# A gated mix of a long convolution and dilated window attention on one core: 64-key by 57-query attention blocks, k and v loaded once, gate in result order, q scaled on VectorE, two-pass last stage

## The chip, the cores and the metric

One core of a Trainium2 chip runs the kernel. The metric is device microseconds of one execution; the kernel before has a median of 310.66 us over three runs (309.36 to 315.1). Its engines are named as in the profile: PE (TensorE matmul) and PEld (TensorE weight load), DVE (VectorE), ACT (ScalarE), POOL (GpSimd), SP (the queue that issues most DMAs).

## What is computed

Everything is bf16, S = 2048 rows, D = 640 columns, 32 heads of 20.

```python
g = sigmoid((x * gate_w).sum(-1, keepdims=True))        # x = A_q
k_shift = sum over lag j = 0..3 of k[n - j] * shift_k[:, j]
kv = k_shift * v
y  = irfft(rfft(pad(kv)) * rfft(pad(ssm_k)))[:S] + kv * ssm_D
a  = x * y
q, k, v = split_heads(x @ wqkv)                         # 32 heads of 20
# row s attends to rows s, s-2, ..., s-14 (W = 8, dilation 2); rows below 0 are masked
o  = softmax(q . k * 20**-0.5) . v
b  = o @ wo
out = g * a + (1 - g) * b
```

## The kernel before: tiling, staging and order

**Attention.** Dilation 2 splits the rows into even and odd ones; each half becomes a window of 8 neighbours. `transposes` writes x transposed into `xT`, the even half and then the odd half, each with 7 rows of zeros ahead. The 2062 columns are cut into 17 blocks of 128 keys and 121 queries (`NB`, `BP`). `vproj` projects v per block (L428) into `VW` with a column of ones (or zeros, `valid`) per head, which gives the softmax sum. `qkproj` projects q and k for 128 features at a time (`ft` 0 to 4, `w` 0 for q and 1 for k; L479), copies them to a staging tile `stg` (two of them, one for q and one for k), and `fragger` copies each head's 20 rows from there by DMA (L513) into `kb` and `qb`, four heads to a tile, where 11 more rows hold a mask in factored form; there are three such pairs of tiles, so the pair of head group t waits until group t-3 has been scored. `score_gen` (L537) multiplies `kb` and `qb` block by block into PSUM, one head's scores on 128 partitions; ACT takes the exponential into `ET` (L544); `pv_gen` (L569) multiplies by `VW`, and DVE divides by the sums (L581, L583) into `oS`.

**Convolution.** `conv` on DVE (L389 to L399) makes kv from k and v, which `loads` brings in four pieces of 16 rows by 160 columns (runs of 320 bytes), reusing two k buffers and one v buffer. The FFT is matrix products: stage 1 (`s1_unit`, L600) and stage 2 (`s2_unit`, L618), first of the filter `h_lin` (`h_stream`) and then of kv (`u_stream`), in five column groups of 16 (`NG`, `IL`); `swaps` and `mults` form the complex product on DVE (L711, L714), `inverse1` is the first inverse stage (L728) into `Cm`, and `final` the last (L811), three time slots of 16 at once. `final` then multiplies by `qg` (L819), which is x times g, adds `bl`, which is (1-g)b from `outproj` (L751, L767, L772), with L822, and writes out (L824).

**Gate.** 80 matmuls (L441) give the gate with rows in `xT`'s order; it goes through a DRAM scratch (L450 to L454) to come back in the result's row order as `g_nat`, and `omg` is 1-g.

**Buffers that tie stages.** `oS` takes the place of `xS`; `wo` that of `Wv`; `h_lin` that of `kvin` (the raw k and v), and later `oT`; `qg` that of `kv`, so `qg` loads only when the last stage-1 product of kv has been issued (event `us1`). `h_stream` starts after the `h_lin` loads, the last q/k projection, the last `conv` piece and the gate matmuls, since its tiles lie where `xT`, `Wqk` and `stg` were.

**Order.** A planner (`Plan`) simulates all the streams with assumed costs while the program is built and so fixes the order on each engine: it picks the request that can start first, plus 120 ns per priority step. PE is shared by all stages; PSUM has four slots; DMAs of `loads` and `fragger` stand in one order on SP. POOL's own start-up work (`pool_head`) is in program order: memsets, DMAs of small constants, 24 DMAs of mask rows into `kb` and `qb` (L373, L374).

Of the kernel before, what the change touches and what calls it, by code (L numbers as in the profile page):

```python
# [17 lines left out]
S = 2048  # L18
D = 640
L = 4096  # L20
H = 32
# [4 lines left out]
BP = 121  # L26
NB = 17
# [5 lines left out]
OW = 2062  # L33
KW = 128 * NB
QW = BP * NB
GROUPS = [[0, 1, 2, 3], [4, 5, 6, 7], [8, 9, 10], [11, 12, 13], [14, 15, 16]]
PARTS = [((0, 1), [(0, 8)]), ((2, 3, 4), [(8, 5), (13, 4)])]

NG = 5
IL = 16  # L40

# [5 lines left out]
def fft_consts():  # L47
# [20 lines left out]
    for b in range(64):  # L68
# [4 lines left out]
    return dict(F1b=_np_bf16(F1b.reshape(128, 128)), G=_np_bf16(G), M=_np_bf16(M.reshape(128, 256)),  # L73
                T=_np_bf16(T))


def attn_consts():
    B, C = 256.0, 512.0
    kk = np.arange(128); qq = np.arange(BP)
    kc = kk // 8 - 8; ko = kk % 8; qc = qq // 8 - 8; qo = qq % 8  # L80
    sk = np.where(kc % 2 == 0, 1.0, -1.0); sq = np.where(qc % 2 == 0, 1.0, -1.0)
    mk = np.zeros((NF, 128)); mq = np.zeros((NF, BP))
    mk[0] = kc * kc; mk[1] = kc; mk[2] = 1.0
    mq[0] = -B; mq[1] = B * (2 * qc + 1); mq[2] = -B * (qc * qc + qc) - C / 2
    for v in range(8):
        mk[3 + v] = sk * (ko == v)
        mq[3 + v] = (C / 2) * sq * np.where(v < qo, -1.0, 1.0)
    tot = np.einsum("fk,fq->kq", mk, mq)
    dlt = kk[:, None] - qq[None, :]
    inb = (dlt >= 0) & (dlt <= 7)  # L90
    assert (tot[inb] == 0).all() and (tot[~inb] <= -C / 2).all()
    for m in (mk, mq):
        assert (_np_bf16(m).astype(np.float64) == m).all()
    pos = BP * np.arange(NB)[None, :] - PRE + kk[:, None]
    valid = (((pos >= 0) & (pos < 1024)) | ((pos >= HS) & (pos < HS + 1024))).astype(np.float32)
    return dict(mk=_np_bf16(np.tile(mk, (1, NB))), mq=_np_bf16(np.tile(mq, (1, NB))),
                valid=_np_bf16(valid), ident=_np_bf16(np.eye(128)))
# [28 lines left out]
class Req:  # L126


    def __init__(self, engs, cost=0.0, deps=(), take=0, give=(), n=0, move=0.0, pri=None):
        self.engs, self.cost, self.deps, self.take, self.give, self.n, self.move = engs, cost, deps, take, give, n, move  # L130
        self.pri = pri


LAT = {("P", "A"): 230.0, ("P", "D"): 230.0, ("A", "P"): 120.0, ("D", "P"): 120.0, ("A", "D"): 100.0, ("D", "A"): 100.0}


class Plan:


    def __init__(self, nslots):  # L140
        self.at = dict(P=0.0, A=0.0, D=0.0, G=0.0, S=0.0)
        self.pipe = 0.0
        self.lane = {"S": [], "G": []}
        self.slots = [Bank() for _ in range(nslots)]
        self.streams = []

# [3 lines left out]
    def cost(self, r, e):  # L150
        if r.n:
            return 190.0 + 0.834 * r.n if e == "A" else 150.0 + 1.05 * r.n
        return r.cost[e] if isinstance(r.cost, dict) else r.cost

    def start(self, r, e):
        t = self.at[e]
        for d in r.deps:
# [6 lines left out]
        if r.move and len(self.lane[e]) >= 8:  # L164
            t = max(t, self.lane[e][-8])
        return t
# [4 lines left out]
    def run(self):  # L171
        while self.streams:
# [9 lines left out]
            assert pick is not None, [s[2].engs for s in self.streams]  # L182
# [5 lines left out]
            self.at[e] = end  # L188
            if r.move:
# [8 lines left out]
            for s in r.give:  # L198
                self.slots[s].free = Ev(end, e)
            try:  # L200
# [6 lines left out]
def kernel(  # L207
# [41 lines left out]
    kvin = p0.tile([128, 2 * 19 * 160 + 16 * 160], BF, name="kvin", tag="H")  # L249
    kv = p0.tile([128, 2, 64, 80], BF, name="kv", tag="kv")  # L250
    G = p0.tile([128, 32, 2, 128], BF, name="G")
    Dz = p0.tile([128, 160], BF, name="Dz")
    F1b = p0.tile([128, 128], BF, name="F1b")
    M = p0.tile([128, 2, 128], BF, name="M")
    g_nat = p0.tile([128, 16], F32, name="g_nat")
    omg = p0.tile([128, 16], F32, name="omg")
    g_chk = p0.tile([128, 16], F32, name="g_chk")
    dpool = ctx.enter_context(tc.tile_pool(name="scratch_dram", bufs=1, space=DRAM))
    g_scr = dpool.tile([S], F32, name="g_scr")
    valid = p0.tile([128, NB], BF, name="valid")  # L260
    wg = p0.tile([128, NDT], BF, name="wg")
    rds = []
    for e in range(2):
        rdb = p0.tile([128, 3, 32], F32, name=f"rd{e}")
        rds.append(rdb)
# [3 lines left out]
    VW = pR.tile([128, NB, H, 21], BF, name="VW")  # L269
# [5 lines left out]
    NET = 8  # L275
    for e in range(NET):
        ETb = pR.tile([128, 2, 512], BF, name=f"ET{e}")
        ETs.append(ETb)
    Lx = ExitStack()
# [3 lines left out]
    pa = pL.tile([128, 16, 160], BF, name="pa")  # L283
    pb = pL.tile([128, 16, 160], BF, name="pb")
    wraw = pL.tile([128, 160, 4], BF, name="wraw")
    wl = pL.tile([128, 4, 160], BF, name="wl")
# [3 lines left out]
    kin = [kvin[:, 3040 * e:3040 * e + 3040].rearrange("p (n c) -> p n c", n=19) for e in range(2)]  # L290
    vin = kvin[:, 6080:8640].rearrange("p (n c) -> p n c", n=16)
# [12 lines left out]
    def us(nbytes, run):  # L304
        return nbytes / 16.0 / run * (10.0 + run / 24.0)
# [3 lines left out]
    def loads():  # L309
        def load(name, dst, src, nb, run, deps=()):  # L310
            g = yield Req("S", 60.0, deps, move=us(nb, run))
# [3 lines left out]
        def load_x(c):  # L315
            yield from load(f"x{c}", xS[:, 4 * c:4 * c + 4, :], xq4[:, c // 2, 4 * (c % 2):4 * (c % 2) + 4, :], 655360, 1280)

        def load_kv(a):
            dk = [ev(f"conv{a - 2}")] if a >= 2 else []
            dv = [ev(f"conv{a - 1}")] if a >= 1 else []  # L320
            for q in range(4):
                lo = 3 if a == 0 else 0
                n0 = 16 * a - 3 + lo
                yield from load(f"k{a}{q}", kin[a % 2][32 * q:32 * q + 32, lo:19, :],
                                raw(k2, n0 * D + 160 * q, [[64 * D, 32], [D, 19 - lo], [1, 160]]), 32 * 19 * 320, 320, dk)
            for q in range(4):
                yield from load(f"v{a}{q}", vin[32 * q:32 * q + 32], raw(v2, 16 * a * D + 160 * q, [[64 * D, 32], [D, 16], [1, 160]]),
                                32 * 16 * 320, 320, dv)

        yield from load("ident", ident[:], ca["ident"].ap(), 32768, 256)  # L330
        yield from load_x(0)
        yield from load("Wv", Wv[:], W3[:, :, 2, :], 819200, 1280)
# [3 lines left out]
        yield from load_kv(0)  # L336
        for w in range(2):
            yield from load(f"W{w}", Wqk[:, :, w, :], W3[:, :, w, :], 819200, 1280)
        for a in range(1, 4):
            yield from load_kv(a)  # L340
        yield from load("G", G[:], cf["G"].ap().rearrange("p (a r b) -> p a r b", a=32, r=2), 2097152, 16384)
        h_lin = p0.tile([128, 80, 2, 64], BF, name="h_lin", tag="H")
        st["h"] = h_lin
        for q in range(4):
            for c in range(2):
                yield from load(f"h{q}{c}", h_lin[32 * q:32 * q + 32, :, c, :],
                                raw(A_ssm_k, (160 * q + 80 * c) * S, [[64, 32], [S, 80], [1, 64]]), 327680, 128, [ev("conv3")])
        wo = p0.tile([128, NDT, D], BF, name="wo", tag="wo")
        st["wo"] = wo
        yield from load("wo", wo[:], B_wo.rearrange("(t p) n -> p t n", p=128), 819200, 1280, [ev("vproj")])  # L350

    st = {}

    def pool_head():
        for c0, c1 in ((0, PRE), (HS, HS + PRE), (2 * HS, XW)):
            nc.gpsimd.memset(xT[:, :, c0:c1], 0.0)
        for q in range(4):
            nc.gpsimd.dma_start(wraw[32 * q:32 * q + 32], raw(A_shift_k, 640 * q, [[0, 32], [4, 160], [1, 4]]))
        nc.gpsimd.memset(kin[0][0:1, 0:3, :], 0.0)
        for q in range(1, 4):  # L360
            nc.gpsimd.memset(kin[0][32 * q:32 * q + 1, 0:3, :], 0.0)
        for q in range(4):
            nc.gpsimd.dma_start(kin[0][32 * q + 1:32 * q + 32, 0:3, :],
                                raw(k2, 61 * D + 160 * q, [[64 * D, 31], [D, 3], [1, 160]]))
        nc.gpsimd.dma_start(valid[:], ca["valid"].ap())
        nc.gpsimd.dma_start(wg[:], gate_w.rearrange("(t p) -> p t", p=128))
        nc.gpsimd.tensor_copy(VW[:, :, :, DH], valid[:].unsqueeze(2).to_broadcast([128, NB, H]))
        for e in range(NET):
            nc.gpsimd.memset(ETs[e][:], 0.0)
        nc.gpsimd.memset(Dz[:], 0.0)  # L370
        for e in range(3):
            for h4 in range(4):
                nc.gpsimd.dma_start(ksets[e][32 * h4 + DH:32 * h4 + DH + NF, :], ca["mk"].ap())  # L373
                nc.gpsimd.dma_start(qsets[e][32 * h4 + DH:32 * h4 + DH + NF, :], ca["mq"].ap())  # L374
        for q in range(4):
            nc.gpsimd.dma_start(Dz[32 * q:32 * q + 1, :], A_ssm_D[160 * q:160 * q + 160].unsqueeze(0))
        nc.gpsimd.dma_start(F1b[:], cf["F1b"].ap())
        nc.gpsimd.dma_start(M[:], cf["M"].ap().rearrange("p (a b) -> p a b", a=2))
# [3 lines left out]
    def conv():  # L382
        yield Req("D", 800.0, [Ev(9000.0)])
        nc.vector.tensor_copy(wl[:], wraw[:].rearrange("p c j -> p j c"))
        for a in range(4):
            k_, dk = kin[a % 2], [ev(f"k{a}{q}") for q in range(4)]

            def tap(dst, j):
                nc.vector.tensor_tensor(dst[:], k_[:, 3 - j:19 - j, :], wl[:, j, :].unsqueeze(1).to_broadcast([128, 16, 160]), ALU.mult)  # L389

            yield Req("D", 1490.0, dk)
            tap(pa, 3)
            for j in (2, 1, 0):
                yield Req("D", 1490.0)
# [490 lines left out]
```

## Time and profile before

| what | value |
|---|---|
| median of three runs | 310.66 us (309.36 to 315.1) |
| span of the profiled execution | 312.3 us, 10653 instructions |
| PE busy / mean granted clock | 236.8 us (76%) / 0.828 of full |
| PEld, DVE, ACT, POOL busy | 166.3, 177.4, 166.4, 71.4 us |
| DMA traffic | 35.46 MB, mean 114 GB/s |
| matmuls: scores L537, times v L569, stage 1 of kv L600, last stage L811 | 544, 544, 160, 512 |
| exponentials L544 | 80, together 64.8 us |
| qg scaling on POOL L793 | 16, together 29.8 us |

The window view of the profile gives, for a stretch of time, each engine's busy time with its number of instructions in brackets, then the granted TensorE clock as a fraction of full speed, the mean busy share of the 16 DMA engines and the GB/s moved. In the timeline and the chain a line is: start, duration, engine, source line, what is written from what. "Idle before" names what ended an engine's wait.

### The profile page before, as it was taken

Reading aid. Unit: us, or ns where it says so; the run is one execution under the profiler, and the core shown is the slowest. Engines: PE = TensorE matmul, PEld = TensorE weight load, DVE = VectorE, ACT = ScalarE, POOL = GpSimd, SP = SyncE. Lnnn points to the kernel's source line nnn. Section 1 sums busy time; section 2 is a strip of 40 time slices with the busy share of each in tenths; the row PEclk is TensorE's granted clock in tenths of the full one; section 3 lists DMA queues with packets and bytes.
Section 4 is the critical chain, followed back from the end, with each engine's and each line's share of the span. In section 5 each row is a group of like instructions: output and inputs, shape, how many; then the busy total and the mean of one; then the engine's idle time right before and its main releaser. Section 6 shows DMA issues by size and latency. Waiting matters only on the chain.

```text
span 312.3 us, 10653 instructions
## 1 busy us (share of the span) xinstructions
PE 236.8 (76%) x4820; PEld 166.3 (53%) x4825; DVE 177.4 (57%) x195; ACT 166.4 (53%) x198; POOL 71.4 (23%) x84
## 2 busy tenths in 40 slices
PE   2897999348987849989888867999999888552210
PEld 2464555324555424536676757878787777541100
DVE  0339696997523124325777977854071577707563
ACT  1244642256489024668987867877878773330000
POOL 8649555100201100000000000000000000089990
PEclk9999999755985778959855879999999997796555
DMA  7999997959639954132300480001406049912343
GB/s 221 242 168 266 154 151 171 186 117 268 178 43 185 176 140 101 28 69 66 73 3 4 97 178 4 5 4 37 104 2 138 2 106 228 217 65 65 86 107 85
DMA packets 49934, 35.46 MB, mean 114 GB/s; under 512 B 41816, under 2 KB 46556, under 8 KB 48864
## 3 DMA queue, kind: packets, MB, share of 16 engines
q1 hardware_dynamic: 47392, 31.91, 49.2%
q0 software_dynamic: 1920, 1.55, 3.2%
q10 hardware_dynamic: 576, 1.31, 1.8%
q8 instruction: 38, 0.62, 0.8%
q14 instruction: 8, 0.07, 0.1%
HBM read 21.44 MB, written 2.63 MB: 77 GB/s over the span
## 4 chain that ended last, share of the span: by engine, by line
PE 46%; SPq 13%; DMA 12%; POOL 8%; ACT 7%; DVE 6%; issue 4%; POOLq 1%; ACTq 0%
PE pj L479 13%; POOL qg L793 8%; SPq L312 8%; PE op L767 7%; PE s L618 5%; DMA qg<-in_A_q_dram 5%; PE sc L537 4%; PE i L728 4%; SPq L513 4%; ACT ET L544 4%; PE O L569 4%; DMA qb<-stg 4%; PE psv L428 3%; PE s L600 3%; DMA Wqk<-in_B_wqkv_dram 2%
## 5 line engine op out<-in xcount | busy, mean ns | idle before, releaser
L544 ACT ACTIVATE ET<-sc 128x726 bf16<-128x726 f32 (+1 forms) x80 | 63.6, 863 | 21.3 <-PE sc L537 20.8
L793 POOL TENSOR_SCALAR qg<-qg,g_nat 128x640 bf16<-128x640 bf16 x16 | 29.8, 1873 | 165.5 <-PE i L728 165.5
L479 PE MATMUL pj<-xT,Wqk 128*128 128x363 bf16 (+3 forms) x250 | 58.9, 388 | 7.4 <-DVE stg L236 5.3
L479 PEld LDWEIGHTS <-Wqk 128*128 128x128 bf16 x250 | 25.3, 108 | 31.1 <-issue 15.2
L537 PE MATMUL sc<-qb,kb 31*128 31x121 bf16 x544 | 29.1, 256 | 12.7 <-ACT ET L544 4.7
L234 ACT CAST Am<-s 128x1024 bf16<-128x1024 f32 x32 | 31.4, 1021 | 5.2 <-PE s L600 5.0
L618 PE MATMUL s<-Am,G 64*128 64x64 bf16 x1280 | 28.8, 198 | 5.8 <-issue 3.3
L537 PEld LDWEIGHTS <-kb 31*128 31x128 bf16 x544 | 16.6, 107 | 26.1 <-issue 20.8
L618 PEld LDWEIGHTS <-G 64*128 64x128 bf16 x1280 | 24.9, 100 | 9.8 <-issue 8.0
L234 ACT CAST stg<-pj 128x968 bf16<-128x968 f32 (+5 forms) x16 | 12.7, 807 | 31.1 <-DMA qb<-stg 13.4
L428 PE MATMUL psv<-Wv,xT 128*128 128x512 bf16 (+1 forms) x165 | 27.4, 314 | 1.2 <-DVE xT L236 1.0
L728 PE MATMUL i<-M,Hs 128*128 128x128 bf16 x160 | 24.7, 245 | 3.4 <-DVE Hs L711 3.4
L728 PE MATMUL i<-M,Hw 128*128 128x128 bf16 x160 | 24.1, 243 | 2.6 <-DVE Hw L714 2.5
L236 DVE CAST stg<-pj 128x726 bf16<-128x726 f32 (+4 forms) x14 | 11.3, 810 | 25.1 <-DMA qb<-stg 12.2
L767 PE MATMUL op<-wo,oT 128*32 128x512 bf16 (+1 forms) x640 | 25.4, 304 | 0.0
L234 ACT CAST Cm<-i 128x1024 bf16<-128x1024 f32 x17 | 17.2, 1012 | 15.0 <-PE i L728 15.0
L711 DVE TENSOR_TENSOR Hs<-Up,Hs 128x2048 bf16<-128x2048 bf16 x10 | 12.2, 1221 | 21.1 <-ACT Up L234 21.0
L728 PEld LDWEIGHTS <-Hs 128*128 128x128 bf16 x160 | 21.8, 153 | 4.5 <-DVE Hs L711 3.6
L728 PEld LDWEIGHTS <-Hw 128*128 128x128 bf16 x160 | 21.8, 154 | 3.1 <-DVE Hw L714 3.1
L236 DVE CAST Hs<-s 128x1024 bf16<-128x1024 f32 x17 | 20.2, 1220 | 5.3 <-PE s L618 5.1
L234 ACT CAST VW<-psv 128x640 bf16<-128x640 f32 x17 | 11.8, 697 | 20.8 <-PE psv L428 20.8
L428 PEld LDWEIGHTS <-xT 128*128 128x128 bf16 x170 | 14.7, 102 | 14.2 <-issue 3.9
(62 smaller groups left out, 335.9 us busy)
## 6 DMA issues: line engine op xcount, KB each, us to landing
Hw<-Hs SPq DMA_DIRECT2D x10, 512.0 KB
xS<-in_A_q_dram SPq DMA_DIRECT2D x4, 640.0 KB
kvin<-in_A_v_dram SPq DMA_DIRECT2D x16, 160.0 KB
h_lin<-in_A_ssm_k_dram SPq DMA_DIRECT2D x8, 320.0 KB
qg<-in_A_q_dram SPq DMA_DIRECT2D x4, 640.0 KB
kb<-stg SPq DMA_DIRECT2D x28, 85.0 KB
kvin<-in_A_k_dram SPq DMA_DIRECT2D x12, 190.0 KB
qb<-stg SPq DMA_DIRECT2D x28, 80.4 KB
```

The lines of the kernel that those rows point to most:

```text
L234: nc.scalar.copy(dst, src)
L236: nc.vector.tensor_copy(dst, src)
L312: nc.sync.dma_start(dst, src)
L428: nc.tensor.matmul(ps[:, n0:n1], lhsT=xT[:, dt, BP * b:BP * b + 128], rhs=Wv[:, dt, n0:n1], start=(dt == 0), stop=(dt == NDT - 1))
L479: nc.tensor.matmul(ps[:, i, 0:n], lhsT=Wqk[:, dt, w, 128 * ft:128 * ft + 128], rhs=rhs, start=(dt == 0), stop=(dt == NDT - 1))
L513: nc.sync.dma_start(dst[r0:r0 + fb - fa, 0:wd], stg[fa - f0:fb - f0, 0:wd])
L537: nc.tensor.matmul(sc[:, hh, BP * bb:BP * bb + BP], lhsT=kb[r:r + DH + NF, 128 * b:128 * b + 128], rhs=qb[r:r + DH + NF, BP * b:BP * b + B ...
L544: nc.scalar.activation(ETs[e][:, :, 0:nw], sc[:, :, 0:nw], ACT.Exp, scale=SCALE)
L618: nc.tensor.matmul(o, lhsT=G[rows, j, rr, :], rhs=Am[rows, 2 * j + rr, :, :], start=(rr == 0), stop=(rr == 1), tile_position=(64 * c, 0), ...
L728: nc.tensor.matmul(o, lhsT=src[:, c, :, :, 8 * oc + il].rearrange("p q j -> p (q j)"), rhs=M[:, k, :], start=(k == 0), stop=(k == 1), skip ...
L767: nc.tensor.matmul(op[32 * gg:32 * gg + 32, n0:n1], lhsT=raw(a, HS * (t % 2) + t // 2 + 8 * gg, [a.ap[0], [32, 32]]), rhs=wo[:, ft, n0:n1] ...
L793: nc.gpsimd.tensor_scalar(qg[:, t, :], qg[:, t, :], g_nat[:, t:t + 1], None, ALU.mult)
```

## The change

- Blocks of 57 queries and 64 keys (`BQ`, `BK`), 18 per row half, 36 in all. Two heads' scores stand on partitions 0 to 63 and 64 to 127, so an exponential covers both. 1152 score matmuls and 1152 times `VW`, each on a part of the array (32 rows by 64 columns, 64 by 64).
- k and v are loaded in two halves of 16 rows by 320 columns (runs of 640 bytes), v straight into `kv`; `conv` works in place in 8 steps of 4 rows, and its taps read `wl[:, 3 - j]` in place of `wl[:, j]`.
- Small start-up loads go to ACT's queue. POOL fills the mask rows of all `kb` and `qb` by broadcasting copies of one tile `mm`, ahead of its memsets of `VW` and `ET`.
- `stg` has three buffers; a projection has two pieces of six blocks per PSUM slot. `h_stream` also waits for the last fragment DMA (`frags`). `wo`, `G` (now in four parts) and `h_lin` are issued as background: low priority, and not before the planner's DMA pipe has nearly run dry.
- Gate matmuls (320, each 32 rows wide) give the result's row order at once; the scratch is gone.
- Stage 1 of kv uses 32x32 tiles: 1280 matmuls in 10 units in place of 160 in 20.
- x is scaled on DVE. The last stage runs twice: columns of groups 0 to 2 (four passes of 4 time slots), then groups 3 and 4 (two of 8); only the second part writes out.
- The planner has new costs, a charge for changing the array's mode, and priority 2 for `conv` (before 0).

```diff
-BP = 121
-NB = 17
+BQ = 57
+BK = 64
+NBP = 18
+NB = 2 * NBP
...
     def start(self, r, e):
         t = self.at[e]
+        if e == "P" and r.mode != self.mode:
+            t += SWITCH
...
+        if r.bg is not None:
+            t = max(t, self.pipe - r.bg)
...
+        def load_rows(name, dst, src, r0, r1, off):
+            for rho in range(4):
+                gg, ch = rho // 2, rho % 2
+                lo = -3 if (r0 == 0 and off and gg == 1) else r0
+                yield from load(f"{name}{rho}", dst[32 * rho:32 * rho + 32, lo + off:r1 + off, :],
+                                raw(src, (32 * gg + lo) * D + 320 * ch, [[64 * D, 32], [D, r1 - lo], [1, 320]]),
+                                (r1 - lo) * 32 * 640 / 200.0)
...
-        yield from load_kv(0)
-        for w in range(2):
-            yield from load(f"W{w}", Wqk[:, :, w, :], W3[:, :, w, :], 819200, 1280)
-        for a in range(1, 4):
-            yield from load_kv(a)
+        yield from load_rows("kA", kin, k2, 0, 16, 3)
+        yield from load("W0", Wqk[:, :, 0, :], W3[:, :, 0, :], 2400.0)
+        yield from load_rows("vA", kv, v2, 0, 16, 0)
+        yield from load("W1", Wqk[:, :, 1, :], W3[:, :, 1, :], 2400.0)
+        yield from load_rows("kB", kin, k2, 16, 32, 3)
+        yield from load_rows("vB", kv, v2, 16, 32, 0)
...
+        for e in range(3):
+            nc.gpsimd.tensor_copy(ksets[e][:].rearrange("p (b k) -> p b k", k=BK), mm[:, 0:BK].unsqueeze(1).to_broadcast([128, NB, BK]))
+            nc.gpsimd.tensor_copy(qsets[e][:].rearrange("p (b k) -> p b k", k=BQ), mm[:, BK:BK + BQ].unsqueeze(1).to_broadcast([128, NB, BQ]))
...
+            def score(dst, rg, b):
+                r = 32 * rg
+                nc.tensor.matmul(dst, lhsT=kb[r:r + DH + NF, BK * b:BK * b + BK], rhs=qb[r:r + DH + NF, BQ * b:BQ * b + BQ],
+                                 start=True, stop=True, tile_position=(r, 64 * (rg // 2)), skip_group_check=True)
...
+                                nc.tensor.matmul(O[64 * sg:64 * sg + 64, half, c0:c0 + 21],
+                                                 lhsT=ET[64 * half:64 * half + 64, hl, BQ * (b % 8):BQ * (b % 8) + 64],
+                                                 rhs=VW[64 * half:64 * half + 64, b, 2 * t + hl, :], start=True, stop=True,
+                                                 tile_position=(64 * half, 64 * sg), skip_group_check=True)
...
+    def s1u_unit(g, qp, Am, free):
+        r = yield Req("P", 128 * 7.5 + 30.0, [], take=2, mode="u")
...
+                    nc.tensor.matmul(pss[bank // 2][o:o + 32, bank % 2, 64 * k:64 * k + 64], lhsT=kv[rows, :, cp], rhs=F1b[rows, 64 * ch:64 * ch + 64],
+                                     start=True, stop=True, tile_position=(32 * rho, o), skip_group_check=True)
...
     def h_stream():
-        yield Req("G", 1000.0, [ev(f"h{q}{c}") for q in range(4) for c in range(2)] + [ev("qk"), ev("conv3"), ev("gatePE")])
+        yield Req("G", 1000.0, [ev(f"h{q}{c}") for q in range(4) for c in range(2)] + [ev("qk"), ev("conv"), ev("gatePE"), ev("frags")])
...
     def qscale():
         for t in range(16):
-            r = yield Req("G", 800.0, [ev("qg"), ev("gate")])
+            r = yield Req("D", 230.0, [ev("qg"), ev("gate")])
             qg = st["qg"]
-            nc.gpsimd.tensor_scalar(qg[:, t, :], qg[:, t, :], g_nat[:, t:t + 1], None, ALU.mult)
+            nc.vector.tensor_scalar(qg[:, t, :], qg[:, t, :], g_nat[:, t:t + 1], None, ALU.mult)
...
     def final():
+        for (g0, g1), m in (((0, 3), 4), ((3, NG), 8)):
+            i0, ni = IL * g0, IL * (g1 - g0)
+            for t0 in range(0, 16, m):
...
```

## The prediction

> **What bounds the kernel now.** I read the windows by stage first, then the chain of waits from its end, then SP's queue, then the durations by shape.
>
> ```profile
> core 0: us, PE busy (x) PEld busy (x) DVE busy (x) ACT busy (x) POOL busy (x), PEclk, DMA share, GB/s
> 36.00:52.00 16.00, 15.89 (x101) 8.83 (x102) 11.84 (x8) 7.51 (x11) 8.46 (x18) 1.00 1.07 147
> 60.00:90.00 30.00, 22.20 (x281) 12.55 (x277) 20.94 (x22) 16.00 (x21) 1.80 (x2) 0.69 0.69 164
> 90.00:150.00 60.00, 49.21 (x658) 27.75 (x655) 20.58 (x37) 33.99 (x43) 2.96 (x5) 0.77 0.54 104
> 150.00:175.00 25.00, 21.95 (x581) 17.45 (x579) 19.99 (x29) 21.18 (x28) 0.00 (x0) 0.59 0.12 26
> 190.00:255.00 65.00, 63.54 (x1725) 52.12 (x1726) 33.99 (x31) 51.36 (x58) 0.00 (x0) 1.00 0.17 38
> 280.00:312.00 32.00, 5.26 (x320) 3.31 (x320) 19.23 (x30) 0.00 (x0) 24.55 (x14) 0.55 0.35 84
> ```
>
> Four stages with four limits. Up to about 60 us the DMA engines are full (share above 1), and at 147 GB/s. From 60 to 150 nothing is full and the PE clock is down. From 150 to 175 ACT and PE take turns at a clock of 0.59. From 190 to 255 PE is 98% busy at full clock. After 280 only POOL works steadily.
>
> ```profile
> 255.54 0.69 SPq L783
> ...
> 258.75 15.81 DMA qg<-in_A_q_dram
> ...
> 274.77 9.33 POOL qg L793 x5
> ...
> 285.96 16.74 POOL qg L793 x9
> ...
> 302.72 2.36 DVE qg L819 x4
> ```
>
> So the end is a chain that hangs on one event, the last stage-1 matmuls of kv (`us1`) at 255: load qg, scale it on POOL, multiply, write, 57 us in all.
>
> ```profile
> 79.46 4.99 SPq L513 DMA_DIRECT2D kb<-stg  x6
> 84.56 20.53 SPq L312 DMA_DIRECT2D h_lin<-in_A_ssm_k_dram  x8
> 105.14 1.46 SPq L312 DMA_DIRECT2D wo<-in_B_wo_dram  x1
> 106.65 0.58 SPq L513 DMA_DIRECT2D kb<-stg  x1
> ```
>
> This is what holds 60 to 150: the head fragments stand on SP behind other loads, here 22 us behind the filter, and PE waits for what they free or fill. Stage 1 of the filter (L600) has no matmul before 150 and 76 in 150 to 175. I therefore write the span as three lengths: start of the filter transform H0 = 150, then 105 to `us1`, then 57 = 312.3 us, and cost the change in each.
>
> ```profile
> L544 ACT ACTIVATE ET<-sc 128x726 bf16<-128x726 f32 x48 | 34.9, 782 | 5.5 <-PE sc L537 5.2
> L544 ACT ACTIVATE ET<-sc 128x968 bf16<-128x968 f32 x32 | 29.9, 984 | 15.9 <-PE sc L537 15.6
> L819 DVE TENSOR_TENSOR qg<-i,qg 128x480 bf16<-128x480 f32 x20 | 11.7, 649 | 15.8 <-POOL qg L793 15.8
> L822 DVE TENSOR_TENSOR qg<-qg,bl 128x1920 bf16<-128x1920 bf16 x5 | 6.1, 1212 | 0.2
> 288.40 1.22 PE L811 MATMUL i<-Cm,T 32*32 32x160 bf16 x94 [0.82 <-DVE qg L819]
> 89.18 0.96 PE L569 MATMUL O<-VW,ET 128*128 128x21 bf16 x32
> ```
>
> **Part 1, up to H0.** *Loads.* k and v are 5.6 MB and run at the 147 GB/s of 36 to 52 us: 38 us. The nearest row for longer runs is 4.5 to 22 us, mostly 1,280-byte runs, 235 GB/s: 22 us. For 640 bytes I take the middle, 190 GB/s, 28 us; gain 10 (2 to 16). The Trainium skill (DMA: Bandwidth & Descriptors, Specifications) puts line rate at runs of 512 B and more; by it the loads would take the 22 us and H0 come 6 us sooner. The 24 mask DMAs were most of queue 0, 3.2% of 312.3 = 10 us of all 16 engines; they go: gain about 8. The start-up DMAs that move to ACT's queue stand ahead of the first xT copy, at 8.07 now; fifteen issues of 0.5 (POOL's constant rows) to 1.5 (POOL's kvin rows) us end at 8 to 22, but DVE shares these copies: 0 to 3 us, I take 1. The first fragments now land at 55 (8 us more for k); I expect about 50.
>
> *Mask fill.* POOL copies 3 x (2304 + 2052) = 13,068 elements per partition. Rows: the ET memset has 0.92 ns per element (941 for 1024), the POOL scaling 2.9 (1872 for 640), the strided VW copy 4.8 (2592 for 544): 12, 38 or 62 us. I take 38, being a plain copy with one input: done at 43, the ET memsets (8 x 0.94) at 51, ahead of the first exponential, now at 66 and then near 56. With 62 the exponentials wait until 70: that loses 14, and is in the high end.
>
> *SP.* 72 fragments by about 0.75 us = 54 us; the filter 20.5, wo 1.5, G 2. From 45 that queue is through at 123 if it never idles, at 108 if part of the filter hides beneath the fragments. The background rule moves G, wo and the filter past fragments, but they still need the same ring before H0, so I credit no more than that.
>
> *PE.* q/k projection: 104k columns in place of 106k, five of 512 take 1.09 us, so 44 either way. Scores: now 22 ns each (16 in 0.35), 12 us; times v: 28 ns (32 in 0.90), 15 us. After: 1152 each. The nearest rows for tiles that run beside each other are L811's 94 (1.22 less the 0.31 of a lone one, 9.8 ns at half clock) and L618's 32 in 0.57, 18 ns. I take 10: 11.5 + 11.5 us, 4 less than now; with 18 it is 41, 14 more. The gate has 320 in place of 80, +1 us (0 to 4). From 45 on: 40 + 23 + 3 = 66, so 111 at full clock, 135 at the 0.73 seen from 60 to 150.
>
> *ACT.* The two exponential rows give 176 ns + 0.835 per element; 32 of 912 and 8 of 456 cost 30.0 + 4.5 = 34.4 in place of 64.8. These 30 us are hidden until 150 (50 of 90 busy); in 150 to 175 they are the path. DVE's conv stays: 2560 elements in 1.49, 64 half-size steps near 0.75, 48 as before; the division is 1440 columns per group for 1360.
>
> *The added wait* (`frags`) stands on POOL ahead of the Dz addition; nothing else is queued there, and PE's stage 1 waits for it. The last fragments were issued at 149 to 155, with projections ending at 149, so it costs the 5 to 8 us of the last copies. H0: queue 108 to 123, PE 111 to 135. I take 118 (108 to 140).
>
> **Part 2, H0 to `us1`.** 105 us now: 25 in which L537 and L569 take 14.1 of PE's 22, 15 to 190, then 65. With `frags` before H0 nearly all scores are done, so these 40 us become about 27: the 40 evictions of the filter at 1.1 us on two engines are 22. Stage 1 of kv was 20 units of 0.47 us (8 matmuls each) = 9.4; after, 10 units of 128: at 7 to 9.8 ns and the 0.25 fixed part, 11 to 15. The weights are strided: the same loads of kv take 178 ns where h_lin's take 109; by that factor 16 ns and 23 us. I take 12. So 27 + 65 + 3 = 95 (86 to 106); I use 93, as outproj may start sooner.
>
> **Part 3, after `us1`.** qg lands 19.5 later as now (229 GB/s, share 0.99 in 258 to 274). Scaling on DVE: 640 elements in 493 is the add row's short form, the most; a quarter of that would be the least; 0.3 x 16 = 5 (2 to 8). First columns: 8 products of 768 from PSUM at 142 + 1.056 each = 0.95, and 4 adds of 1536 at 1.0: 11.6. Second: 4 x 1.22 + 2 x 1.3 = 7.5. DVE ends at 43.6. Its cover is gone: POOL's 29.8 leave, but 24 us of DVE stand behind the same load. Cm is complete at 21.6 and T lands near 21.7, both hidden. Then the write: now each sixth goes out as it is done, and 160 KB are left, 4.6 us from the last add. After, two writes of 1.31 MB, at 229 GB/s 5.7 us each, the first from 39.9: about 3.5 + 11.4 later, 55. So the tail gains 2 only (48 to 58). I take 54.
>
> Sum: 118 + 93 + 54 = 265 us of span; the median stood to the profiled span as 310.66 to 312.3, so **264 us**.
>
> **Rivals.** *Small matmuls cost more than these rows say* (ends slower). 3,584 of them (1152 + 1152 + 1280) are at 10 ns in the sum. Each ns more is 3.6 us. At L618's 18 ns: 264 + 29 = 293. It is slower than before from 310.7 = 264 + 3.6 x 13, that is 23 ns each. For it: PE is 98% busy where half of them stand. Against: L811's 9.8 ns at half clock. The Trainium skill (TensorE: Matmul & The Clock Gate, "Wait — 56ns, not 53.3ns?") gives 25 ns start to start as the least at any width; L811's row is far under that, and by the rule the time would be 264 + 54 = 318.
>
> *H0 does not move*: the mask fill is slow, or the background filter goes last behind `frags`; H0 stays at 135 to 145, which gives 280 to 290. For it: a clock of 0.69 to 0.77 in this stretch. Against: 30 us less ACT and three staging tiles where ACT's and DVE's copies now wait 13.4 and 12.2 us for fragments.
>
> *All packs well*: H0 108, 88, tail 50: 245.
>
> **Chances.** The forecast (252 to 276) 0.5; packs well 0.2; H0 stays 0.2; small matmuls 0.1, a third of it beyond 311. Range 243 to 290: it leaves out the dearest small matmuls and the least of the good case. Two per cent, 6 us, is about what these runs (309 to 315) can tell: faster 0.92, same 0.04, slower 0.04.
>
> **What would show it.** First L600 matmul near 118; exponentials 34 us; `us1` near 211; qg scaled on DVE within 8 us; after the last add 9 to 12 us of writes only. Wrong if scores or stage 1 of kv take over 15 ns each, if POOL still fills masks past 55, or if PE idles before the filter with the fragments done.

## The result, and the profile after

The changed kernel takes 350.94 us (median; 349.37 to 352.19) beside 312.88 for the kernel before, timed with it: it is 38 us slower by the medians, and the ratio is 1.129, 95% interval 1.120 to 1.138. Some executions are slower whatever the kernel, so the ratios, and the differences given below, are of the runs within 1.5% of a kernel's fastest. The forecast was 264 us, 243 to 290. Its profiled execution has a span of 350.1 us. In the forecast's three lengths: the filter transform (now L620) starts at 165.0, not 118; `us1` follows 106.7 us later (the q load is issued at 271.7), not 93; the tail is 78.4 us, not 54. The errors are 47, 14 and 24 us.

The page's engine totals, PE clock and instruction queue (packets, MB, share):

```profile
PE 251.0 (72%) x8158; PEld 198.0 (57%) x8158; DVE 176.1 (50%) x218; ACT 145.6 (42%) x172; POOL 24.7 (7%) x30
PEclk9999999958589898555787998998989977855855
q8 instruction: 63, 1.03, 1.3%
```

PE now issues 8,158 matmuls, each with a weight load (4,820 before). The last line is what to see: the queue that brings the program's instructions moved 63 packets of 16 KB. 16,316 PE instructions in 63 blocks is about 256 a block, that is 128 matmuls with their weight loads. Before it was 38.

The windows of before, and the end, in the changed kernel:

```profile
core 0: us, PE busy (x) PEld busy (x) DVE busy (x) ACT busy (x) POOL busy (x), PEclk, DMA share, GB/s
36.00:52.00 16.00, 16.00 (x192) 12.21 (x189) 13.59 (x17) 7.92 (x12) 0.00 (x0) 1.00 0.92 182
60.00:90.00 30.00, 20.88 (x840) 15.90 (x838) 20.38 (x28) 12.75 (x18) 0.00 (x0) 0.76 0.51 134
90.00:150.00 60.00, 46.52 (x1487) 31.64 (x1490) 25.81 (x47) 23.75 (x30) 0.00 (x0) 0.78 0.44 86
150.00:175.00 25.00, 17.21 (x800) 15.34 (x793) 12.60 (x19) 15.24 (x18) 0.95 (x1) 0.58 0.39 64
190.00:255.00 65.00, 55.57 (x2086) 46.88 (x2084) 29.64 (x26) 35.37 (x38) 0.00 (x0) 0.95 0.16 36
303.00:350.00 47.00, 16.18 (x905) 14.27 (x904) 24.84 (x33) 4.05 (x4) 0.00 (x0) 0.58 0.25 58
```

Loads run at 182 GB/s where 147 stood, and from 60 on ACT has less to do; but there nothing is full. From 190 to 255, where PE was 98% busy, it idles 9 of 65 us; in 60 to 90 it idles 9 of 30 (8 before), with three times the matmuls of before. What ends PE's idle time (total us, times, longest):

```profile
PE i L856 <- issue: 10.3, 6, 2.5
PE O L587 <- issue: 9.7, 6, 2.2
PE s L664 <- issue: 8.2, 6, 3.3
PE op L810 <- issue: 8.2, 3, 5.1
...
PE sc L543 <- issue: 5.8, 4, 2.0
...
PE gps L454 <- issue: 5.4, 3, 3.1
```

"issue" means that PE waited for nothing that the profile shows. All such rows sum to 55.9 us; before they were two of any size, 8.0 us in all. The gate in PE's timeline (start, length) shows the pattern:

```profile
66.50 2.00 PE L454 MATMUL gps<-wg,xT 128*32 128x1 bf16 x128 [0.27 <-issue]
70.50 2.01 PE L454 MATMUL gps<-wg,xT 128*32 128x1 bf16 x128 [2.01 <-issue]
75.60 0.45 PE L454 MATMUL gps<-wg,xT 128*32 128x1 bf16 x19 [3.09 <-issue]
```

Exactly 128 matmuls, a pause of 2 to 3 us, 128 matmuls. The end of the chain of waits has the same rhythm in the last inverse stage (L856), where nothing hides it:

```profile
326.28 2.20 PE i L856 x247
328.48 2.06 issue
330.54 1.29 PE i L856 x128
331.83 2.17 issue
333.99 1.27 PE i L856 x122
335.27 2.48 issue
```

Hence **theory 1**: PE's program arrives in blocks of 128 matmuls; a block takes some 3.7 us to come, and small matmuls use one up in 1.3 to 2. **Theory 2**: the array itself is slower on small tiles, at switches of tile size or a low clock. **Theory 3**: the planner charged 7.5 to 9.5 ns per small matmul and so made a bad order.

### The profile page after: what moved, and what is told of

Same layout as the page of the kernel before. It is cut to its first block, busy times and chain, and to the rows that moved or that the text cites. A ratio compares the mean times of both kernels' runs of the same rounds, so it can differ in the third digit from the quotient of the medians.

```text
span 350.1 us, 17133 instructions
## 1 busy us (share of the span) xinstructions
PE 251.0 (72%) x8158; PEld 198.0 (57%) x8158; DVE 176.1 (50%) x218; ACT 145.6 (42%) x172; POOL 24.7 (7%) x30
## 3 DMA queue, kind: packets, MB, share of 16 engines
q10 hardware_dynamic: 1592, 1.89, 2.5%
## 5 line engine op out<-in xcount | busy, mean ns | idle before, releaser
L483 PE MATMUL pj<-xT,Wqk 128*128 128x342 bf16 (+1 forms) x300 | 53.4, 340 | 2.3 <-issue 2.3
L567 ACT ACTIVATE ET<-sc 128x912 bf16<-128x912 f32 (+1 forms) x40 | 32.1, 853 | 31.2 <-PE sc L543 31.0
L810 PE MATMUL op<-wo,oT 128*32 128x128 bf16 (+1 forms) x640 | 31.0, 349 | 8.2 <-issue 8.2
L248 ACT CAST stg<-pj 128x684 bf16<-128x684 f32 (+1 forms) x25 | 19.0, 761 | 34.2 <-PE pj L483 27.9
L440 PE MATMUL psv<-Wv,xT 128*64 128x320 bf16 x360 | 28.1, 319 | 5.3 <-ACT xT L248 3.9
L771 PE MATMUL i<-F,Hw 128*128 128x128 bf16 x160 | 24.0, 244 | 5.4 <-DVE Hw L757 5.4
L440 PEld LDWEIGHTS <-xT 128*64 128x64 bf16 x360 | 21.4, 117 | 11.0 <-ACT xT L248 4.4
L810 PEld LDWEIGHTS <-oT 128*32 128x32 bf16 x640 | 17.6, 142 | 17.0 <-issue 12.9
L543 PE MATMUL sc<-qb,kb 31*64 31x57 bf16 x1152 | 17.9, 208 | 10.4 <-issue 5.8
L771 PE MATMUL i<-F,Hs 128*128 128x128 bf16 x160 | 24.4, 246 | 0.2 <-DVE Hw L757 0.2
L643 PE MATMUL s1u<-F,kv 32*32 32x64 bf16 x1280 | 21.3, 217 | 3.5 <-issue 3.5
L643 PEld LDWEIGHTS <-kv 32*32 32x32 bf16 x1280 | 19.6, 144 | 5.2 <-issue 4.6
```

The lines of the kernel that those rows point to most:

```text
L248: nc.scalar.copy(dst, src)
L440: nc.tensor.matmul(ps[64 * o:64 * o + 64, i, 0:320], lhsT=xT[:, dt, s0:s0 + BK], rhs=rhs, start=(dt == 0), stop=(dt == NDT - 1), tile_posi ...
L483: nc.tensor.matmul(ps[:, i, 0:n], lhsT=Wqk[:, dt, w, 128 * ft:128 * ft + 128], rhs=xT[:, dt, s0:s0 + n], start=(dt == 0), stop=(dt == NDT ...
L543: nc.tensor.matmul(dst, lhsT=kb[r:r + DH + NF, BK * b:BK * b + BK], rhs=qb[r:r + DH + NF, BQ * b:BQ * b + BQ], start=True, stop=True, tile ...
L567: nc.scalar.activation(ETs[e][:, :, 0:BQ * nb], scs[k][:, :, 0:BQ * nb], ACT.Exp, scale=SCALE)
L643: nc.tensor.matmul(pss[bank // 2][o:o + 32, bank % 2, 64 * k:64 * k + 64], lhsT=kv[rows, :, cp], rhs=F1b[rows, 64 * ch:64 * ch + 64], star ...
```

## The experiments

The changed kernel was timed in another batch than its variants, and the kernel before was timed in each. A difference from the changed kernel's 350.9 us is therefore followed, in brackets, by the one that the ratios to the kernel before give; the two are up to 4 us apart, and no difference here is surer than that.

**Matmuls alone** (zeros are written as output).

> A kernel of matmuls alone, with zeros written as output: 1,024 of 32x32 with 64 columns on the 16 tile positions, 1,024 of 64x64 with 21 columns, 512 of 128x128 with 128 columns, 1,024 of 128x128 with 16 columns, and again 1,024 of 32x32 with 64 columns while 7.9 MB are loaded. Theory 1 (PE's instructions arrive as 16 KB blocks of 256, that is 128 matmuls with their weight loads, and the next block takes about 3.65 us): every small form takes about 3.65 us per 128 (29 us per 1,024), whatever its shape, the 128x128x128 form its own 7 us per 128 without stalls, and the stretch beside the loads takes longer, 4 to 5 us per 128. Theory 2 (the array: small tiles, switches of tile size, a low clock): the forms differ, 32x32 with 64 columns near its 10 ns (1.3 us per 128), the others at 15 to 30 ns by their columns, and loads change nothing.

PE's timeline of it (L67 32x32 with 64 columns, L71 64x64 with 21, L74 and L77 128x128 with 128 and 16, L84 as L67 beside the loads):

```profile
13.46 1.89 PE L67 MATMUL p<-x,w 32*32 32x64 bf16 x128 [1.83 <-issue]
17.19 1.89 PE L67 MATMUL p<-x,w 32*32 32x64 bf16 x128 [1.84 <-issue]
...
35.56 1.89 PE L71 MATMUL p<-x,w 64*64 64x21 bf16 x128 [1.84 <-issue]
...
57.65 30.88 PE L74 MATMUL p<-x,w 128*128 128x128 bf16 x512
...
101.26 3.56 PE L77 MATMUL p<-z,w 128*128 128x16 bf16 x128 [0.17 <-issue]
...
132.84 1.89 PE L84 MATMUL p<-x,w 32*32 32x64 bf16 x128 [4.30 <-issue]
```

Both small shapes start a block every 3.73 us (17.19 less 13.46; the others 3.5 to 4.0): 29 ns per matmul, though inside a block one takes 14.8. L74's 512 run 30.88 us, 7.7 per 128, without a pause, and L77's block of 3.56 us pauses 0.17: the next block is brought while one runs, so a block costs the longer of its own time and about 3.7 us. The DMA view has one 16 KB packet of the instruction queue in each period (near 14.5, 18.3 and 22.0 us), some 1.1 us after a block's start and 2.4 to 2.7 before the next; the packet itself is short, and what fills the rest is not shown. Beside loads at some 400 GB/s the pause grows to 4.0 to 4.9 us, and the period to about 6. Theory 2 is out for these shapes; frequent changes between tile sizes were not in this run.

**Stage 1 of kv, fewer and more matmuls in the changed kernel.**

```
-        for k in range(8):  ... rhs=F1b[rows, 64*ch:64*ch+64]   # N = 64
+        ... lhsT=kv[rows, :, cp], rhs=G[rows, 0:2] as 512 columns  # one for eight
```

> The changed kernel, but each unit of stage 1 of kv issues 16 matmuls of 32x32 with 512 columns in place of 128 with 64 (their moving operand is a constant, so the numbers of this stage are others; the columns streamed are the same): 1,120 matmuls fewer, 8.75 blocks of 256 PE instructions. Theory 1: 8.75 x 3.65 = 32 us of loading go, and 15 to 32 us of the time, for the copies out of PSUM bound the stretch next. Theory 2: the array streams the same columns through the same tiles, at most 3 us. Theory 3 (the planner's order, made with 7.5 to 9.5 ns per small matmul): nothing, the order is the same.

Measured 317.76 us (317.32 to 318.19), ratio to the kernel before 1.012 (1.007 to 1.018): 33 us less (36) than the changed kernel for the same columns, 29.6 ns for each matmul left out. The instruction queue has 54 packets, nine fewer, and the "issue" pauses sum to 39.4 us. Theory 1's upper figure.

```
-        for ph in range(4):
+        for ph in [0, 1, 2, 3] * 2:
```

> The changed kernel with each matmul of stage 1 of kv issued twice to the same place: 1,280 more, 10 blocks. Theory 1: 10 x 3.65 = 36 us of loading more, 20 to 37 us of the time, the rest under waits that are there already. Theory 2 at 10 ns each: 12 us. Theory 3: as theory 2.

393.11 us (389.44 to 396.99), ratio 1.242 (1.232 to 1.253): 39 us more (35), 30.5 ns each; 73 packets, ten more. That is about the upper end of theory 1's range, and far from 12.

**The same instructions in another order.**

```
-  8.5 * 4 * ns * nb + 30.0      # scores; likewise PV, kv stage 1, gate, stage 2, last stage
+  28.5 * 4 * ns * nb + 30.0
```

> The changed kernel's own instructions, all of them, in the order that the planner makes when each small matmul is charged 28.5 ns (what it took, loading included) in place of 7.5 to 9.5. Theory 3 (the order was made with wrong costs, and that is what the time went to): 15 to 30 us faster than the changed kernel. Theory 1 (loading of PE's instructions): the same 63 blocks are loaded, whatever their order, so within 6 us of the changed kernel's 351.

347.69 us (344.99 to 350.01), ratio 1.108 (1.098 to 1.118): 3 us less (6.5). In its profile the filter transform starts at 153 and q's load at 261, some 11 us earlier than in the changed kernel, but the span is only 5 us shorter, and the same 63 packets still come with 54.2 us of "issue" pauses. Theory 3 is a small term at most.

**The gate in 128-wide weights.**

```
-  for gg in range(4): ... lhsT=raw(a, ... + 8 * gg, [a.ap[0], [32, 32]])
+  ... lhsT=raw(a, ..., [a.ap[0], [8, 128]])
```

> The changed kernel with the gate's 320 matmuls of 32-wide weights replaced by 80 of 128-wide ones (its rows then come in another order, so the gate multiplies other rows): 240 matmuls fewer, 1.9 blocks. Theory 1: up to 1.9 x 3.73 = 7 us, so 4 to 7 us faster than the changed kernel. Theory 2 (32-wide tiles at 10 ns): 0 to 2 us.

343.01 us, ratio 1.094 (1.085 to 1.103): 8 us less (11), 32 ns for each of the 240, a little more than the 7 us that theory 1 gave at most. A part that I had put at "+1 us (0 to 4)" cost 8.

**Attention's second product in half as many.**

```
-  for hl in range(2): ... O[..., c0:c0 + 21], rhs=VW[64 * half:64 * half + 64, b, 2 * t + hl, :]
+  for hl in range(1): ... O[..., c0:c0 + 42], rhs=VW[64 * half:64 * half + 64, b, 2 * t:2 * t + 2, :]
```

> The changed kernel with attention's second product in half as many matmuls: one with 42 columns writes both heads of a pair from the first head's weights, in place of two with 21 (every second head gets the other's weights; the columns streamed are the same): 576 matmuls fewer, 4.5 blocks. It tells whether the loading of attention's matmuls sets the start of the filter transform (165 us in the changed kernel). Theory 1: 4.5 x 3.73 = 17 us of loading go, and 8 to 17 us of the time. Theory 2 (array): 0 to 3. If the queue of fragments sets that start: 0 to 3.

333.14 us, ratio 1.066 (1.055 to 1.078): 18 us less (20), 31 ns each, and the filter transform starts at 149, not 165. SP's timeline of the changed kernel, and then of this one:

```profile
145.07 6.17 SPq L524 DMA_DIRECT2D kb<-stg  x7
151.28 6.15 SPq L319 DMA_DIRECT2D h_lin<-in_A_ssm_k_dram  x4
```

```profile
131.45 5.21 SPq L524 DMA_DIRECT2D kb<-stg  x7
136.71 6.88 SPq L319 DMA_DIRECT2D h_lin<-in_A_ssm_k_dram  x4
```

The last fragments, and the last loads of the filter behind them, come 14 us earlier with no edit to either: this queue followed PE, not PE the queue.

**Halved exponentials in the kernel before.**

```
-  nc.scalar.activation(ETs[e][:, :, 0:nw], sc[:, :, 0:nw], ACT.Exp, scale=SCALE)
+  nc.scalar.activation(ETs[e][:, :, 0:nw // 2], sc[:, :, 0:nw // 2], ACT.Exp, scale=SCALE)
```

> The kernel before with each exponential on half of its columns (the others keep a constant 1): what the 30 us less of ACT are worth where PE's instructions are not more. The prediction's part 1 held them hidden until 150 and on the path from 150 to 175: 5 to 12 us faster than the kernel before. If ACT holds back PE in all of attention (PE waited 12.7 us for ET): 12 to 20. If PE and the queue of fragments set that stage: 0 to 4.

307.29 us, ratio 0.982 (0.973 to 0.991): 6 us faster than the kernel before (3 to 8), with 37.0 us of exponentials in place of 64.8. That is about what the smaller blocks' saving on ACT is worth by itself, and the product above alone gives back three times that. Where it arises is not shown: the profiled run, of 313.7 us, has the filter transform at 152 and q's load at 254.8, where the kernel before has 151 and 255.1.

**The last stage in one pass.**

```
-  for (g0, g1), m in (((0, 3), 4), ((3, NG), 8)):
+  for g0, g1 in ((0, NG),):   # t in steps of 3
```

> The changed kernel with the last inverse stage in one pass, 512 matmuls in place of 1,024 (the part of the change undone). Theory 1: 4 blocks fewer. In the changed kernel the second pass's blocks (330 to 342 us) end the chain; in one pass the 4 blocks are 15 us of loading against 18.7 us of VectorE's products, which begin when the last group's columns are there, at about 326: the end at 348 to 352, so within 4 us of the changed kernel, either way. If two passes pay as meant: 5 to 10 us slower.

339.24 us, ratio 1.085 (1.067 to 1.102): 13 us less (14), where I had expected no more than 4. In its profile the products begin at 313.3, not at the 326 that I had assumed, for no first pass stands ahead of the last group's products with the filter (done at 308, not 321); from there VectorE takes 3.33 us for each three steps of t and never waits for PE. So the 13 us are order and blocks together, and two passes cost where they were to pay.

**The order on VectorE at the end.** VectorE's timeline of the changed kernel:

```profile
300.55 1.23 DVE L754 TENSOR_TENSOR Hs<-Up,Hs 128x2048 bf16<-128x2048 bf16 x1
301.69 4.82 DVE L836 TENSOR_SCALAR qg<-qg,g_nat 128x640 bf16<-128x640 bf16 x16
...
319.60 1.22 DVE L757 TENSOR_TENSOR Hw<-Up,Hw 128x2048 bf16<-128x2048 bf16 x1
330.82 2.36 DVE L863 TENSOR_TENSOR qg<-i,qg 128x1024 bf16<-128x1024 f32 x2 [10.00 <-PE i L856]
```

The last group's first product with the filter is done at 302, its last at 321; between them stand q's scaling and the whole first pass.

```
-  Req("D", 230.0, [ev("qg"), ev("gate")])
+  Req("D", 230.0, [ev("qg"), ev("gate")], pri=5)   # products and adds of the last stage: pri=3
```

> The changed kernel with another order on VectorE at the end: the last group's products with the filter stand ahead of the scaling of q and of the first pass's products. In the changed kernel VectorE waited for PE until 298, then scaled q (5 us) and did the first pass (11 us) before that group's last product at 318.5, which the last inverse matmuls waited for; PE then loaded blocks. If that order costs: the last inverse stage starts 12 to 15 us earlier, and 5 to 12 us of the time go. If the loading for the second pass's 512 matmuls ends last anyway: 0 to 4 us.

347.74 us: three runs at 346.9 to 350.3 and one at 341.28, so whether this order gains 1 to 4 us or 10 stays open. In the profile, of a run of 348.6 us, the four products are done at 306, 15 us earlier, and the last 860 matmuls of the last stage then run block by block from 311 to 334. In that run the blocks end last.

**q scaled on VectorE in the kernel before**, first as the change does it, then behind the last group's products.

```
-  Req("G", 800.0, [ev("qg"), ev("gate")]) ... nc.gpsimd.tensor_scalar(qg...
+  Req("D", 230.0, [ev("qg"), ev("gate")]) ... nc.vector.tensor_scalar(qg...
+  second: Req("D", 380.0, [ev("qg"), ev("gate"), ev(f"mult{NG - 1}")])
```

> The kernel before with one part of the change: q scaled on VectorE. In the tail before, the scalings on GpSimd took 29.8 us and the first final products waited for them 16 us. 16 x 0.38 = 6 us on VectorE stand before the products instead, with the read of q under the forward stages: 6 to 12 us faster (about 303). If the tail's end is held by something else, no change.

> The kernel before with q scaled on VectorE, as b_dve_q, but behind the last group's products with the filter. In b_dve_q the scaling stood ahead of them and waited 11.7 us for the load of q, and these products ran at 278 to 283 and the final ones from 288.9. Now the group's products go at 261 to 266, q's scaling ends at 278 with the load at 273, and the final products begin at 278 to 281: 8 to 11 us faster than the kernel before (about 304). If the gain of this part is not there for another reason (T's load, the final matmuls): 0 to 3 us.

314.12 us, ratio 1.002 (0.996 to 1.008), where 6 to 12 us less were expected, and 304.58 us, ratio 0.968 (0.958 to 0.979). The first has on VectorE

```profile
273.25 4.82 DVE L793 TENSOR_SCALAR qg<-qg,g_nat 128x640 bf16<-128x640 bf16 x16 [11.72 <-DMA qg<-in_A_q_dram]
278.00 1.22 DVE L711 TENSOR_TENSOR Hs<-Up,Hs 128x2048 bf16<-128x2048 bf16 x1
```

and the second

```profile
272.94 1.22 DVE L714 TENSOR_TENSOR Hw<-Up,Hw 128x2048 bf16<-128x2048 bf16 x1
276.61 4.83 DVE L793 TENSOR_SCALAR qg<-qg,g_nat 128x640 bf16<-128x640 bf16 x16 [2.45 <-DMA qg<-in_A_q_dram]
```

The queue runs in order: a scaling that waits for a load holds every product behind it. Behind them it gains some 10 us (7 to 13), all that was expected of the part.

**A mended change.**

```
+  stage 1 of kv: lhsT=kv[64*gg:64*gg+64, :, cp], rhs=F1b[64*gg:64*gg+64, :]   # 640 for 1,280
+  gate: 80 wide matmuls, then one with a permuted identity
+  last stage: for g0, g1 in ((0, NG),): in threes of t
+  qscale waits for mult4; the planner charges 28.5 ns for the first two
```

> The changed kernel, computing all of the reference, with fewer PE instructions: stage 1 of kv in 640 matmuls of 64 rows and 128 columns (1,280 before; the filter's channels are put in the matching order), the gate in 80 wide matmuls and one that permutes its rows, the last inverse stage in one pass, and the scaling of q behind the last group's products with the filter. 1,390 matmuls fewer, 10.9 blocks. Theory 1: 10.9 x 3.73 = 40 us of loading go; of the parts alone, 8 for the gate, 15 to 18 for stage 1, 8 to 14 for the tail: 310 to 325. Theory 2: 335 to 345.

302.22 us (298.78 to 306.92), ratio 0.959 (0.947 to 0.970): 51 us below the changed kernel (53), and all four runs lie below the seven of the kernel before beside them (310.0 to 317.7); 53 packets, pauses of 31.0 us. That is better than the 310 to 325 expected of it, and about as good as the small edit of the kernel before, whose interval overlaps. Of the 53 blocks attention's two products are 18 (2,304 matmuls); 15.2 us of the pauses stand ahead of them.

## Why the prediction was wrong

**The step that failed** is the price of small matmuls: "I take 10" for scores and their product, and "I take 12" us for 1,280 of stage 1. The rows it came from were true but short: L811's 94 in 1.22 us and L618's 32 in 0.57 are less than one block of 128 and hold no pause. Over longer stretches the price is 30 to 32 ns (the four runs that changed little but their number; by the ratios 28 to 34, and 46 for the gate, where 3 us are much), set by the arrival of instructions. The first rival had the right line and too small a chance: with 3,584 at 29.6 ns, 264 + 3.6 x 19.6 = 335 us; at 32, 343. Its own bound, "23 ns each", was passed. It was held down by L811 and by a PE "98% busy"; but that stretch has 1,725 matmuls in 65 us, 4.8 us for 128, and so says nothing of blocks under 3.7 us. What the profile of before did show and I passed over, its instruction packets and two waits on "issue":

```profile
q8 instruction: 38, 0.62, 0.8%
PE sc L537 <- issue: 4.7, 1, 4.7
PE s L618 <- issue: 3.3, 2, 2.2
```

The Trainium skill (Runtime: NRT & Kernel Launch, Instruction fetch mechanics) describes blocks of 16 KiB or 256 instructions, fetched while the current one runs, and calls the cost "mostly hidden". The block size agrees with 63 packets for 16,316 instructions; the cost is hidden only behind matmuls whose block takes over 3.7 us, and here left PE idle 55.9 us.

**The 85 us by place.** Of the span's error (350.1 less 265), "issue" accounts for 23.2 us before the filter transform, 13.6 to `us1` and 19.1 in the tail: 55.9.
- *H0*, 47: from 45 us on PE idled 28.7 us (the 23.2, and 4.2 for fragments) and was busy for 91.3, where 118 leaves 73. The projections took 53.4 from there on, where the sum has 40: PE was busy for 146 ns per matmul of theirs at a granted clock of 1.00 (45 to 60) and about 190 at 0.73 to 0.84 (60 to 150). So the 135 of "111 at full clock, 135 at the 0.73" was the better bound. Scores and their product were busy for 17.9 and 16.2 us (11.5 each said). The clock's part was read from the trace and not tried alone.
- *`us1`*: 106.7 less 13.6 is the 93 that was forecast. With wide matmuls in stage 1 this stretch was 82.6 us, 24 less, where the sum has 12 for all of stage 1.
- *Tail*: the scaling took 4.8 us (5 said), the first pass 11 (11.6), the writes 8.4 after the last add (9 to 12). "24 us of DVE stand behind the same load" missed that the last group's products queue behind them, and that the second pass loads four blocks with nothing beside it.

**What held.** The exponentials fell to 32.1 us (34.4 said), and their 30 us were mostly hidden, as said: 28 us less of them gave 6 us alone. POOL's mask copies took 12 us, the low end (38 taken), so the second rival's slow fill had no ground; its other branch, the filter's loads last behind the fragments, did come about, but as an effect of PE. The convolution's steps took 0.82 us each where 0.75 was taken, with no effect found on the end. One small slip: at 235 and 190 GB/s the 5.6 MB of k and v take 24 and 29 us, not 22 and 28.

## What to carry to other kernels

Count the instructions of an unrolled engine program as a load: here 128 matmuls with their weight loads cost the longer of their own time and 3.7 us, and about 6 beside heavy loads. A split into more, smaller matmuls pays only where something else on PE covers the blocks, and a price per matmul must be read from a stretch longer than a block. When work moves to another engine, place it by the slowest thing that it waits for: the same scaling gave 0 us ahead of the products and about 10 behind them.

## What the runs showed of the hardware

- Inside a block, 128 small matmuls took 1.89 us at a granted clock of 1.00 (windows at 6 to 57 us of the matmuls alone) and 1.89 at 0.50 (120 to 155): there neither the clock nor the columns (64 or 21) set their pace. In the changed kernel's last stage 128 took 1.29 us; why is open.
- The pauses grew under DMA traffic: 1.84 us alone, 4.0 to 4.9 us beside loads, 1.6 to 2.1 again once these were over, and 5.1 us in the changed kernel ahead of L810, while q was loaded.
- Not tried: a loop over the same code, and small matmuls spread among large ones so that each block holds both.
